# The first batch's last two token tiles in 64 by 64 tiles, and two steps moved ahead of the projection's second part

## The chip, the cores and the metric

The kernel runs on one core of a Trainium2 chip. The metric is device time in microseconds, of the whole launch; lower is better. TensorE (PE in the profile), VectorE (DVE), ScalarE (ACT) and GpSimd (POOL) each work through a queue of their own in program order and wait for each other by semaphores; SyncE (SP) issues most of the DMAs.

## What is computed

An attention whose keys and values are first squeezed to 32 slots, followed by a mixture of eight experts of which each token takes the best one:

```python
a = softmax(phi, over the sequence)                  # (8 batches, 8 heads, 576, 32)
k_m = einsum('bhsm,bhsd->bhmd', a, k)                # 32 slots per head
v_m = einsum('bhsm,bhsd->bhmd', a, v)
attn = softmax(q @ k_m.T / 8)                        # (8, 8, 576, 32)
x = (attn @ v_m) as (4608 tokens, 512)
logits = normalized(x) @ normalized(expert_emb).T / tau
e = argmax(logits); gate = softmax(logits)[e]
out = gate * (relu(x @ w1[e]) @ w2[e])               # w1 (8, 512, 1024), w2 (8, 1024, 512)
```

All is float32.

## The kernel before, in words

The eight batches are worked off one after the other by `batch` (L821), called from L1069. A batch has 576 tokens in five tiles of 128 that start at 0, 128, 256, 384 and 512 (the last has 64, and holds them twice). The 8 heads lie in two groups g of four, 32 slots each, so a group fills 128 partitions.

The attention weights of a batch stand in `aw` (slot by token). `attend` (L108) multiplies them with `vv`, which holds per head the products of values with each other and with the eight expert vectors: the columns of the experts, added over heads, are the logits, and the other columns serve the norm of a token. In batch 0 `attend` makes a 128-row matmul per tile and group (L119), `turned` (L166) transposes the tile's weights by PE and ACT copies them to `ea`, DVE adds the logits (L124), and `best` (L157) finds the maximum and the one-hot `oh`. `norm` (L175) multiplies and sums on DVE. In the later batches `open` and `pairs` (L127, L131) do the same products in 64 by 64 tiles, four per tile and group into four PSUM tiles, with 72 columns each; there the logits lie in two halves (h) that are added (L154), the transposed weights come by DMA, and the norm sums lie in two halves `s2`.

`choose` votes for the batch's most frequent expert and loads its w1. `project` (L655) multiplies the squeezed values with w1, in two halves k of 512 columns: 16 small matmuls, cast by ACT to `gh`, and the rest subtracted by DVE to `gl`. `part` (L637) splits `aw` in the same way, high part by ACT, low part by POOL. `first` (L670) is the first layer: 16 steps, for two halves s of the tokens and eight blocks f of 128 hidden units, six matmuls each (L681), then ACT's relu (L684, for s = 1 a second one, L686) and DVE's rest `hl` (L687), which is the last to read the step's PSUM tile. `mm` hands out four PSUM tiles in rotation, `pt` four others. Blocks f 0 to 3 need only the first half of `gh` and `gl`. `second` (L692) is the second layer, 40 places in eight-step tiles: tile 4 first, with h4 and w2 in float32 (L723), then tiles 0 to 3 with the split weights `wh`, `wl` (L734).

`split_w` (L648) makes one of the eight weight halves `wh` (cast) and `wl` (POOL subtract, L652).

The order of everything around these loops is written by hand: `steps` (L743) fills lists `first[n]` and `second[n]` with calls that are issued after the n-th step, in the order in which they were appended. For batch 0 before the change: weight splits 0 and 1 in first[2], splits 2 to 7 in first[9] to first[14] (the first six on POOL alone, 6 and 7 with ACT's cast); tiles 3 and 4 in first[2], their norm in first[3], the count `total` in first[4], the six parts of `late` (root of the norm, gates) in first[3] to first[8]. Of these six the first is L238, L38 and L39 on DVE, the next three are three operations each of the root, with two more in the fourth, the fifth is L254 to L256, and the sixth is ACT's exponential L258, DVE's L261 and L262, POOL's write of `idx` (L263) and three more on DVE. The scores of batch 1 come in first[9]. The softmax of batch 2's phi (two maxima L457 on DVE, two exponentials L472 on ACT) is at second[18] and second[21] of batch 0, ahead of `visit` at second[24], which transposes it (`flip`, L497) and then makes batch 1's products.

Ahead of the first layer of batch 0 the order is: first half of the projection, `part` for tokens 128 to 287, keys and values of batch 1, tiles 1 and 2 with their transposes, second half of the projection, `part` for tokens 288 to 575, norm of tiles 1 and 2.

Of the kernel before, what the change touches and what calls it, by code (L numbers as in the profile page):

```python
# [8 lines left out]
F32 = mybir.dt.float32  # L9
# [37 lines left out]
class Tokens:  # L47


    def __init__(self, k, b, pt):  # L50
        self.k, self.nc, self.b, self.pt = k, k.nc, b, pt
        wk = k.wk.tile
        self.lg = wk([P, NT, E], F32, tag="lg", name=f"lg{b}")
        self.ss = wk([P, NT], F32, tag="ss", name=f"ss{b}")
        self.s2 = wk([P, 2, NT], F32, tag="s2", name=f"s2{b}") if b else None
        self.m = wk([P, NT], F32, tag="m", name=f"m{b}")
        self.oh = wk([P, NT, E], BF16, tag="oh", name=f"oh{b}")
        self.po = {}
# [49 lines left out]
    def attend(self, *ti, pt=None, turned=True):  # L108

        k, nc, b = self.k, self.nc, self.b  # L110
        if b:
            self.open()
            self.pairs()
            return
        for i in ti:
            self.po[i] = po = (pt or self.pt)([P, NC * (D + E)], f"po{b}_{i}")
            to = slice(T0[i], T0[i] + P)
            for g in range(NG):
                nc.tensor.matmul(po[:, 144 * g : 144 * g + P + E], lhsT=k.aw[:, g, to], rhs=k.vv[:, g], start=True, stop=True)  # L119
        if turned:  # L120
            self.turned(*ti)
        for i in ti:
            e = self.po[i].rearrange("p (g m) -> p g m", g=NG)[..., D : D + E]
            nc.vector.tensor_reduce(out=self.lg[:, i], in_=e.rearrange("p g e -> p e g"), axis=AX.X, op=ALU.add)  # L124
        self.best(*ti)

    def open(self):  # L127

        self.ps = [self.pt([P, 512], f"po{self.b}_{n}") for n in range(4)]

    def pairs(self):  # L131
# [3 lines left out]
        for i in range(NT):  # L135
# [11 lines left out]
        self.room = ps[-1][:, 512 - E :]  # L147
        l2 = k.wk.tile([P, NT, E], F32, tag="l2", name=f"l2{b}")
        for n, i in enumerate((slice(0, 3), slice(3, NT))):
# [4 lines left out]
        nc.vector.tensor_tensor(out=self.lg, in0=self.lg, in1=l2, op=ALU.add)  # L154
        self.best(*range(NT))
# [19 lines left out]
    def norm(self, *ti):  # L175
        k, nc = self.k, self.nc
        for i in ti:
            x = k.ea[:, i].rearrange("p (g k m) -> p g k m", g=NG, k=2)
            po = self.po[i] if self.b else [self.po[i].rearrange("p (g k m) -> p g k m", g=NG, k=2)[..., :D]]
            for h, y in enumerate(po):  # L180
                to = x[:, :, h] if self.b else x
# [8 lines left out]
                    accum_out=(self.s2[:, h] if self.b else self.ss)[:, i : i + 1],  # L190
# [42 lines left out]
    def root(self):  # L233
        k, nc, b, ss = self.k, self.nc, self.b, self.ss
        self.n = n = k.wk.tile([P, NT], F32, tag="n", name=f"n{b}")
        if b:
            nc.vector.tensor_tensor(out=ss, in0=self.s2[:, 0], in1=self.s2[:, 1], op=ALU.add)
# [38 lines left out]
class Kernel:  # L276
# [466 lines left out]
    def steps(self, b, t, u):  # L743
# [7 lines left out]
        if not b:  # L751
            late = t.late()
            first[2].append(lambda: t.attend(3, 4))
            first[3].append(lambda: t.norm(3, 4))
            first[4] += [t.total, lambda: self.load_kv(2)]

            for f in range(3, 9):
                first[f].append(lambda: next(late))
            first[12] += [lambda: self.keep(0), lambda: self.load_q(2)]
        if u:  # L760
# [19 lines left out]
            if m < B:  # L780
                for g in range(NG):
                    second[11 + 3 * g + o].append(lambda g=g: self.softmax(m, (g,)))
# [38 lines left out]
    def batch(self, b, t, u):  # L821
# [11 lines left out]
        for k, _ in enumerate(self.project(b, self.vT[b % 2]) if u else ()):  # L833
            if not b:
                for g in range(NG):
                    self.part(g, slice(HS, S) if k else slice(P, HS), self.nc.scalar.copy)
                if k:
                    t.norm(1, 2)
                else:
                    self.keys(1)  # L840
                    self.values(1)
                    t.attend(1, 2)
        if b and u:

            self.scores(b + 1)
# [255 lines left out]
```

## Time and profile before

| | us |
|---|---|
| median of 3 runs | 406.81 (405.87 to 408.75) |
| the profiled execution | 406.74 |
| its span, first to last instruction | 404.9 |
| PE busy | 393.5 (97% of the span) |
| DVE busy | 262.3 (65%) |
| POOL busy | 171.2 (42%) |
| ACT busy | 157.2 (39%) |

The granted TensorE clock of the profiled execution is 0.998 of full. The span and the engine times come from the page's first part. Times in rows are us from the start of the span. A row of a timeline has start, duration, engine, line, operation, tile written and tiles read, the shape, how many equal instructions are merged in it, and in brackets the idle time before it with what ended it. Matmuls overlap, so a merged row lasts a little longer than the distance to the next one.

### The profile page before, as it was taken

The page shows a single profiled execution, that of the slowest core. Times are in us where ns is not written, and L with a number is a line of the kernel's source. Part 1 is how long each engine was busy: PE and PEld are TensorE (multiplying, and loading weights), DVE is VectorE, ACT ScalarE, POOL GpSimd, SP SyncE. Part 2 cuts the span into 40 slices and gives each one's busy share as a digit, 9 for nine tenths or more (in the row PEclk, how much of TensorE's full clock was granted, in tenths as well). Part 3 has the DMA queues.
Part 4 walks back from the last instruction along what each step waited for, and adds up shares of the span by engine and source line. Part 5 has one row for each costly group of instructions (what it writes and reads, how often), then busy time and mean ns, then how long its engine had stood idle before and what let it go on. Part 6 is the DMA issues. An engine that isn't in the chain of part 4 may idle for free. (4 is left out here: it accounts for less than half of the span.)

```text
span 404.9 us, 10350 instructions
## 1 busy us (share of the span) xinstructions
PE 393.5 (97%) x3933; PEld 318.5 (79%) x3933; DVE 262.3 (65%) x909; ACT 157.2 (39%) x430; POOL 171.2 (42%) x205
## 2 busy tenths in 40 slices
PE   7889999999999999999999999999999999999995
PEld 3458877798777978879787888879788897879784
DVE  4698795769664794758855795747936595745000
ACT  4366623165313633147311753137231561146110
POOL 1036563187133940369121961349303681329300
PEclk9999999999999999999999999999999999999999
DMA  8999927995679925995469926798359404790011
GB/s 265 345 363 357 375 61 183 342 358 212 149 255 386 349 46 132 346 384 234 74 215 389 387 82 160 251 388 338 56 137 361 178 2 81 249 396 6 14 53 56
DMA packets 69862, 91.24 MB, mean 225 GB/s; under 512 B 41800, under 2 KB 47688, under 8 KB 69808
## 3 DMA queue, kind: packets, MB, share of 16 engines
q1 hardware_dynamic: 66928, 82.00, 60.9%
q0 software_dynamic: 2688, 8.26, 5.8%
q8 instruction: 32, 0.52, 0.5%
q10 hardware_dynamic: 192, 0.28, 0.2%
q14 instruction: 22, 0.18, 0.1%
HBM read 71.19 MB, written 19.33 MB: 224 GB/s over the span
## 5 line engine op out<-in xcount | busy, mean ns | idle before, releaser
L681 PE MATMUL ph<-aT,gh 128*128 128x288 f32 x512 | 103.2, 297 | 0.0
L734 PE MATMUL py<-wh,hh 128*128 128x512 f32 x248 | 99.3, 400 | 0.0
L734 PE MATMUL py<-wh,hl 128*128 128x512 f32 x248 | 96.7, 390 | 0.0
L734 PE MATMUL py<-wl,hh 128*128 128x512 f32 x248 | 96.7, 390 | 0.0
L652 POOL TENSOR_TENSOR wl<-w2s,wh 128x512 fp32r<-128x512 f32 x64 | 85.1, 1330 | 5.0
L681 PEld LDWEIGHTS ph<-aT,gh 128*128 128x128 f32 x512 | 81.8, 188 | 1.7 <-DVE oh L162 0.8
L681 PE MATMUL ph<-aT,gl 128*128 128x288 f32 x256 | 75.4, 294 | 0.0
L687 DVE SCALAR_TENSOR_TENSOR hl<-ph,hh 128x288 fp32r<-128x288 f32 x128 | 55.8, 450 | 22.1 <-ACT hh L684 16.7
L739 ACT ACTIVATE ys<-py,gate 128x512 f32<-128x512 f32 (+1 forms) x39 | 25.1, 642 | 105.3 <-PE py L734 70.3
L684 ACT ACTIVATE hh<-ph 128x288 fp32r<-128x288 f32 x128 | 52.4, 417 | 31.9 <-PE ph L681 31.6
L868 POOL DMA_DIRECT2D out_dram<-ys x28 | 15.5, 553 | 106.1 <-ACT ys L739 69.4
L734 PEld LDWEIGHTS py<-wh,hh 128*128 128x128 f32 x248 | 46.5, 188 | 14.6 <-issue 4.9
L734 PEld LDWEIGHTS py<-wh,hl 128*128 128x128 f32 x248 | 46.6, 188 | 10.1
L734 PEld LDWEIGHTS py<-wl,hh 128*128 128x128 f32 x248 | 46.6, 188 | 9.0
L681 PEld LDWEIGHTS ph<-aT,gl 128*128 128x128 f32 x256 | 48.0, 188 | 0.0
L642 POOL TENSOR_TENSOR aT<-aw,aT 128x576 fp32r<-128x576 f32 (+3 forms) x20 | 23.7, 1204 | 48.4 <-DVE aT L641 42.8
L651 POOL CAST wh<-w2s 128x512 fp32r<-128x512 f32 x62 | 38.6, 622 | 1.0 <-DMA w2s<-w 0.9
L723 PE MATMUL py<-w2s,h 128*64 128x256 f32 x256 | 29.4, 382 | 0.0
L665 DVE TENSOR_TENSOR gl<-pg,gh 128x512 fp32r<-128x512 f32 x32 | 20.0, 684 | 8.7 <-ACT gh L664 8.7
L723 PEld LDWEIGHTS py<-w2s,h 128*64 128x64 f32 x256 | 17.7, 137 | 9.3 <-DVE hl L687 1.0
L472 ACT ACTIVATE ex<-ex,nm 128x576 f32<-128x576 f32 x16 | 12.3, 771 | 29.5 <-DVE nm L457 29.5
L664 ACT CAST gh<-pg 128x512 fp32r<-128x512 f32 x32 | 16.5, 599 | 10.5 <-PE pg L662 10.5
(180 smaller groups left out, 468.9 us busy)
## 6 DMA issues: line engine op xcount, KB each, us to landing
kx<-kv SPq DMA_DIRECT2D x32, 512.0 KB, 7.5
w2s<-w SPq DMA_DIRECT2D x32, 512.0 KB, 9.8
w1s<-w SPq DMA_DIRECT2D x28, 512.0 KB, 6.4
out_dram<-ys POOLq DMA_DIRECT2D x28, 256.0 KB, 6.1
qt<-qT SPq DMA_DIRECT2D x12, 576.0 KB, 8.8
ad<-aw SPq DMA_DIRECT2D x8, 576.0 KB, 12.5
td<-x SPq DMA_DIRECT2D x56, 72.0 KB, 2.1
ea<-td SPq DMA_DIRECT2D x7, 512.0 KB, 4.4
```

The costliest lines, as they stand in the source:

```text
L642: self.nc.gpsimd.tensor_tensor(out=al, in0=a, in1=ah.bitcast(F32), op=ALU.subtract)
L651: (copy or self.nc.scalar.copy)(h, x)
L652: self.nc.gpsimd.tensor_tensor(out=l, in0=x, in1=h.bitcast(F32), op=ALU.subtract)
L664: nc.scalar.copy(self.gh[:, g, f], ps[g])
L665: nc.vector.tensor_tensor(out=self.gl[:, g, f], in0=ps[g], in1=self.gh[:, g, f].bitcast(F32), op=ALU.subtract)
L681: nc.tensor.matmul(p, lhsT=w[:, g, fs], rhs=x[:, g, to], start=g == 0 and k == 0, stop=g == 1 and k == 2)
L684: nc.scalar.activation(self.hh[:, f, to], p, AF.Relu)
L687: nc.vector.scalar_tensor_tensor(out=self.hl[:, f, to], in0=p, scalar=0.0, in1=self.hh[:, f, to].bitcast(F32), op0=ALU.max, op1=ALU.subtract)
L723: nc.tensor.matmul(p[64 * j : 64 * j + 64], lhsT=self.h4[:, f], rhs=self.w2s[:, f, d * j : d * j + d], start=f == 0, stop=f == 7,)
L734: nc.tensor.matmul(p, lhsT=h[:, f, to], rhs=w[:, f], start=f == 0 and k == 0, stop=f == 7 and k == 2)
L739: nc.scalar.activation(y[:, :d], p, AF.Copy, scale=gate[:, i : i + 1])
L868: eng.dma_start(self.out[r : r + P], y)
```

## The change

Batch 0's tiles 3 and 4 go through `open` and `pairs`, which now can begin at tile 3 (two PSUM tiles instead of four), so their products become sixteen 64 by 64 matmuls of 72 columns; the transposes for `ea` follow them. Their logits are two halves that DVE adds (L154), their norms four operations instead of two, and the root begins with an addition of the two halves of `s2`. The calls for tiles 3 and 4, their norm, the count and the six parts of `late` each move one place later, to first[3], first[4], first[5] and first[4] to first[9]. The weight splits stay where they were.

The opening of batch 0 becomes: `part` of group 0 for tokens 128 to 287, first half of the projection, `part` of group 1, keys and values, products and logits of tiles 1 and 2; then step 0 of the first layer, the transposes and norms of tiles 1 and 2, step 1, the second half of the projection, `part` for tokens 288 to 575, step 2 and so on.

In batch 0 the two maxima of batch 2's softmax go to first[13] and first[14] and its exponentials to second[2] and second[5]; in the later batches the softmax is called one place earlier.

```diff
--- before.py
+++ after.py
@@ -52,7 +52,7 @@
         wk = k.wk.tile
         self.lg = wk([P, NT, E], F32, tag="lg", name=f"lg{b}")
         self.ss = wk([P, NT], F32, tag="ss", name=f"ss{b}")
-        self.s2 = wk([P, 2, NT], F32, tag="s2", name=f"s2{b}") if b else None
+        self.s2 = wk([P, 2, NT], F32, tag="s2", name=f"s2{b}")
         self.m = wk([P, NT], F32, tag="m", name=f"m{b}")
         self.oh = wk([P, NT, E], BF16, tag="oh", name=f"oh{b}")
         self.po = {}
@@ -108,9 +108,14 @@
     def attend(self, *ti, pt=None, turned=True):
 
         k, nc, b = self.k, self.nc, self.b
-        if b:
-            self.open()
-            self.pairs()
+        if b or ti[0] == 3:
+            self.open(b)
+            if b:
+                self.pairs()
+            else:
+                self.pairs(1)
+                self.turned(*ti)
+                self.logits(1)
             return
         for i in ti:
             self.po[i] = po = (pt or self.pt)([P, NC * (D + E)], f"po{b}_{i}")
@@ -124,15 +129,15 @@
             nc.vector.tensor_reduce(out=self.lg[:, i], in_=e.rearrange("p g e -> p e g"), axis=AX.X, op=ALU.add)
         self.best(*ti)
 
-    def open(self):
-
-        self.ps = [self.pt([P, 512], f"po{self.b}_{n}") for n in range(4)]
-
-    def pairs(self):
+    def open(self, all=True):
+
+        self.ps = [self.pt([P, 512], f"po{self.b}_{n}") if all or n > 1 else None for n in range(4)]
+
+    def pairs(self, first=0):
 
         k, nc, b, d, ps = self.k, self.nc, self.b, D + E, self.ps
         at = lambda i, h: ps[2 * (i // 3) + h][:, 2 * d * (i % 3) :][:, : 2 * d].rearrange("p (g m) -> p g m", g=NG)
-        for i in range(NT):
+        for i in range(3 * first, NT):
             for g in range(NG):
                 for h, c in ((0, 0), (1, 0), (0, 1), (1, 1)):
                     r, to = slice(64 * h, 64 * h + 64), slice(64 * c, 64 * c + 64)
@@ -145,14 +150,22 @@
                     )
             self.po[i] = [at(i, h)[..., E * h :][..., :D] for h in range(2)]
         self.room = ps[-1][:, 512 - E :]
+        if not first:
+            self.logits()
+
+    def logits(self, first=0):
+
+        k, nc, b, d, ps = self.k, self.nc, self.b, D + E, self.ps
         l2 = k.wk.tile([P, NT, E], F32, tag="l2", name=f"l2{b}")
-        for n, i in enumerate((slice(0, 3), slice(3, NT))):
+        for n in range(first, 2):
+            i = slice(3, NT) if n else slice(0, 3)
             for h, to in enumerate((self.lg, l2)):
                 e = ps[2 * n + h][:, : 2 * d * (i.stop - i.start)].rearrange("p (i g m) -> p i m g", g=NG, m=d)
                 e = e[:, :, D - D * h :][:, :, :E]
                 nc.vector.tensor_reduce(out=to[:, i], in_=e, axis=AX.X, op=ALU.add)
-        nc.vector.tensor_tensor(out=self.lg, in0=self.lg, in1=l2, op=ALU.add)
-        self.best(*range(NT))
+        i = slice(3 * first, NT)
+        nc.vector.tensor_tensor(out=self.lg[:, i], in0=self.lg[:, i], in1=l2[:, i], op=ALU.add)
+        self.best(*range(3 * first, NT))
 
     def best(self, *ti):
 
@@ -176,9 +189,10 @@
         k, nc = self.k, self.nc
         for i in ti:
             x = k.ea[:, i].rearrange("p (g k m) -> p g k m", g=NG, k=2)
-            po = self.po[i] if self.b else [self.po[i].rearrange("p (g k m) -> p g k m", g=NG, k=2)[..., :D]]
+            two = isinstance(self.po[i], list)
+            po = self.po[i] if two else [self.po[i].rearrange("p (g k m) -> p g k m", g=NG, k=2)[..., :D]]
             for h, y in enumerate(po):
-                to = x[:, :, h] if self.b else x
+                to = x[:, :, h] if two else x
                 nc.vector.tensor_tensor_reduce(
                     out=to,
                     in0=y,
@@ -187,7 +201,7 @@
                     scalar=0.0,
                     op0=ALU.mult,
                     op1=ALU.add,
-                    accum_out=(self.s2[:, h] if self.b else self.ss)[:, i : i + 1],
+                    accum_out=(self.s2[:, h] if two else self.ss)[:, i : i + 1],
                 )
 
     def count(self, pt, name, ti):
@@ -233,8 +247,8 @@
     def root(self):
         k, nc, b, ss = self.k, self.nc, self.b, self.ss
         self.n = n = k.wk.tile([P, NT], F32, tag="n", name=f"n{b}")
-        if b:
-            nc.vector.tensor_tensor(out=ss, in0=self.s2[:, 0], in1=self.s2[:, 1], op=ALU.add)
+        i = slice(0 if b else 3, NT)
+        nc.vector.tensor_tensor(out=ss[:, i], in0=self.s2[:, 0, i], in1=self.s2[:, 1, i], op=ALU.add)
         nc.vector.tensor_scalar(out=ss, in0=ss, scalar1=0.0, scalar2=None, op0=ALU.max)
         for _ in sqrt(nc, k.wk, n, ss, [P, NT], "nr"):
             yield
@@ -750,11 +764,11 @@
             at.append(lambda j=j: self.split_w(self.nc.gpsimd.tensor_copy if b or j < 6 else None))
         if not b:
             late = t.late()
-            first[2].append(lambda: t.attend(3, 4))
-            first[3].append(lambda: t.norm(3, 4))
-            first[4] += [t.total, lambda: self.load_kv(2)]
-
-            for f in range(3, 9):
+            first[3].append(lambda: t.attend(3, 4))
+            first[4] += [lambda: t.norm(3, 4), lambda: self.load_kv(2)]
+            first[5].append(t.total)
+
+            for f in range(4, 10):
                 first[f].append(lambda: next(late))
             first[12] += [lambda: self.keep(0), lambda: self.load_q(2)]
         if u:
@@ -779,7 +793,9 @@
             m = b + 2
             if m < B:
                 for g in range(NG):
-                    second[11 + 3 * g + o].append(lambda g=g: self.softmax(m, (g,)))
+                    if not b:
+                        first[13 + g].append(lambda g=g: self.largest(m, g))
+                    second[10 + 3 * g if b else 2 + 3 * g].append(lambda g=g: self.softmax(m, (g,)))
                 second[16 + o].append(lambda: self.shares(m))
                 second[17 + o].append(lambda: self.visit(u, m))
                 second[(20 if b else 19) + o].append(lambda: self.gather(u, m))
@@ -830,19 +846,22 @@
         if b and u:
             self.keys(b + 1)
             self.values(b + 1)
-        for k, _ in enumerate(self.project(b, self.vT[b % 2]) if u else ()):
-            if not b:
-                for g in range(NG):
-                    self.part(g, slice(HS, S) if k else slice(P, HS), self.nc.scalar.copy)
-                if k:
-                    t.norm(1, 2)
-                else:
-                    self.keys(1)
-                    self.values(1)
-                    t.attend(1, 2)
-        if b and u:
-
-            self.scores(b + 1)
+        project = self.project(b, self.vT[b % 2]) if u else ()
+        if b:
+            list(project)
+            if u:
+                self.scores(b + 1)
+        else:
+            self.part(0, slice(P, HS), self.nc.scalar.copy)
+            next(project)
+            self.part(1, slice(P, HS), self.nc.scalar.copy)
+            self.keys(1)
+            self.values(1)
+            t.attend(1, 2, turned=False)
+            first[0] += [lambda: t.turned(1, 2), lambda: t.norm(1, 2)]
+            first[1].insert(0, lambda: list(project))
+            for g in range(NG):
+                first[1].append(lambda g=g: self.part(g, slice(HS, S), self.nc.scalar.copy))
         for n, _ in enumerate(self.first(b)):
             for step in first[n]:
                 step()
```

## Rows read from the trace of the kernel before

**Rows 1.** Waits of PE, 26 to 66 us: engine, line, releaser, total, times, longest.
```profile
PE po L504 <- ACT ex L472: 0.5, 1, 0.5
PE tt L172 <- ACT kT L551: 0.4, 1, 0.4
PE pg L662 <- DMA w1s<-w: 0.3, 1, 0.3
```

**Rows 2.** Windows: stretch, length, busy us (count) of five engines, clock, DMA, GB/s.
```profile
150.00:200.00 50.00, 50.00 (x507) 41.32 (x506) 35.16 (x119) 19.25 (x52) 21.39 (x24) 1.00 0.74 239
```

**Rows 3.** Timeline of PE in the opening, 29 to 37 us.
```profile
29.32 1.09 PE L119 MATMUL po<-vv,aw 128*128 128x136 f32 x8
30.77 0.66 PE L172 MATMUL tt<-ident,aw 128*128 128x128 f32 x4 [0.36 <-ACT kT L551]
31.36 1.09 PE L662 MATMUL pg<-w1s,vT 64*32 64x512 f32 x16
...
34.86 1.09 PE L119 MATMUL po<-vv,aw 128*128 128x136 f32 x8
35.78 0.60 PE L172 MATMUL tt<-ident,aw 128*128 128x128 f32 x4
36.14 0.51 PE L681 MATMUL ph<-aT,gh 128*128 128x288 f32 x2
```

**Rows 4.** Timeline of PE at steps 8 and 9 of the first layer.
```profile
40.83 0.43 PE L681 MATMUL ph<-aT,gh 128*128 128x288 f32 x2
...
41.23 0.52 PE L681 MATMUL ph<-aT,gh 128*128 128x288 f32 x2
```

**Rows 5.** Timeline of DVE, 33 to 41 us.
```profile
33.14 1.29 DVE L665 TENSOR_TENSOR gl<-pg,gh 128x512 fp32r<-128x512 f32 x2 [0.91 <-ACT gh L664]
...
36.61 0.92 DVE L162 TENSOR_TENSOR oh<-lg,m 128x16 bf16<-128x16 f32 x1
...
38.83 0.63 DVE L238 TENSOR_SCALAR ss<-ss 128x5 f32<-128x5 f32 x1
...
39.70 0.17 DVE L39 TENSOR_SCALAR nrg<-nrg 128x5 int32<-128x5 int32 x1
...
40.71 0.45 DVE L687 SCALAR_TENSOR_TENSOR hl<-ph,hh 128x288 fp32r<-128x288 f32 x1
```

**Rows 6.** Timeline of POOL, 34 to 45 us.
```profile
34.00 1.57 POOL L642 TENSOR_TENSOR aT<-aw,aT 128x288 fp32r<-128x288 f32 x2 [2.70 <-ACT aT L641]
...
36.22 1.28 POOL L652 TENSOR_TENSOR wl<-w2s,wh 128x512 fp32r<-128x512 f32 x1
...
38.13 1.30 POOL L652 TENSOR_TENSOR wl<-w2s,wh 128x512 fp32r<-128x512 f32 x1
44.50 0.20 POOL L263 TENSOR_SCALAR idx<-m 128x5 f32<-128x5 f32 x1 [5.07 <-DVE m L262]
```

**Rows 7.** Timeline of PE where batch 0 turns batch 2's softmax, 64 to 66 us.
```profile
64.40 0.28 PE L504 MATMUL po<-ident,ex 64*128 64x64 f32 x2 [0.46 <-ACT ex L472]
...
65.10 1.48 PE L139 MATMUL po<-vv,aw 64*64 64x72 f32 x80
```

**Rows 8.** Timeline of DVE, the two maxima of batch 2's softmax.
```profile
61.98 1.37 DVE L457 TENSOR_REDUCE nm<-ex 128x1 f32<-128x576 f32 x2
```

**Rows 9.** Timeline of DVE, norms of batch 1 in two halves.
```profile
71.86 0.28 DVE L182 CUSTOM_DVE_ANT_1 ea<-po,ea 128x128 f32<-128x128 f32 x1
...
72.07 0.28 DVE L182 CUSTOM_DVE_ANT_1 ea<-po,ea 128x128 f32<-128x128 f32 x1
```

**Rows 10.** Timeline of DVE, one operation of two SBUF inputs at two places.
```profile
140.97 1.12 DVE L73 TENSOR_TENSOR x<-x,mx 128x576 f32<-128x576 f32 x1
...
145.19 0.75 DVE L73 TENSOR_TENSOR x<-x,mx 128x576 f32<-128x576 f32 x1
```

**Rows 11.** Timeline of POOL, the cast beside the first of them.
```profile
140.85 0.61 POOL L651 CAST wh<-w2s 128x512 fp32r<-128x512 f32 x1
```

**Rows 12.** Timeline of ACT, the exponential of batch 0's gates.
```profile
43.74 0.24 ACT L258 ACTIVATE l<-l 128x40 f32<-128x40 f32 x1 [1.79 <-DVE l L256]
```

## The prediction

> **What bounds the kernel now.** I read the waits of TensorE (PE) first. From 26 to 66 us PE stands still three times, 0.5, 0.4 and 0.3 us [rows 1]; after that it is full, as the window from 150 to 200 us shows [rows 2] (the next three windows of 50 us read the same). So the kernel runs as long as PE's own queue, and whatever PE gains or loses in the first batch comes out at the end one to one. Then I read PE's timeline of the opening [rows 3] and around steps 8 and 9 of the first layer [rows 4] (a step is one pass of L681 over six matmuls; 16 per batch, 0 to 15). One thing in rows 4 matters: the pair of matmuls at 41.23 takes 0.52 us where the pair before it takes 0.43. The 0.1 us is a small wait that the waits view does not list. Step 9 writes the PSUM buffer that step 5 used (four in rotation), and VectorE (DVE) reads step 5's buffer at 40.71 for 0.45 us, until 41.16 [rows 5]. So at step 9 DVE is already just late: PE has no slack against DVE there. Last I read DVE beside GpSimd (POOL): the one-hot compare L162 lasts 0.92 us and the maximum L238 0.63 [rows 5], where L39, of the same shape as L238, takes 0.17. Both long ones lie under a POOL subtract L652 and end with it: 37.53 against 37.50, 39.46 against 39.43 [rows 5, 6]. Two engines wait for each other here.
>
> **The change, part by part, on PE.** *Opening.* The products of tiles 1 and 2 start at 29.32 as before and take 0.92 us (by the equal block at 34.86, which gives way to transposes at 35.78) [rows 3]. Before, the transposes then wait 0.36 us for ACT's copy of kT and start at 30.77. Now step 0 stands there, at 30.24. Its last operand, POOL's low part of group 1, starts when ACT has cast group 1, which stays behind two gh casts; I allow 0.1 to 0.2 us. A step costs 0.80 (two spacings of 0.40 in rows 4) and 0.1 more when another kind of matmul stood before it (0.51 against 0.43, at 36.14 and 40.83 [rows 3, 4]). So: step 0 to 31.2, transposes 0.4 to 31.6, step 1 to 32.5, second part of the projection (1.0, plus 0.1) to 33.6, steps 2 and 3 to 35.3.
>
> *Products of tiles 3 and 4.* Eight records in 0.92 become 32. The same shape appears in batch 1: 80 records in 1.48 [rows 7], so 32 take 0.59; with nothing for the changes of shape the gain is 0.33, with two restarts of 0.1 it is 0.13. I take 0.17, nearer the second, since the block stands between two other shapes. Then transposes 0.36: step 4 starts at 36.45, before at 36.14 + 0.9 = 37.0. PE has gained 0.5 to 0.6. (The Trainium skill, TensorEngine Tiling (Array Packing), Tiling Modes, promises four independent 64 by 64 tiles and says that a change of mode drains the engine. At the full four tiles the products would take 0.92 x 72/136 = 0.49, an estimate from that page, and save 0.43; the row says 0.59 before any drain.)
>
> *First batch's softmax for batch 2.* The two maxima (L457, 1.37 us for both) run at 61.98, directly behind DVE's last transpose into aw [rows 8]; PE waits 0.46 us for the exponentials at 64.40 [rows 7]. Put into steps 13 and 14 and the start of the second layer, they are done some 10 us earlier, so the 0.46 goes. What is late next there is the aw that the products at 65.10 read: DVE has it at about 62, so over 3 us are left, and where DVE is late PE is late too. The cost is 1.4 us of DVE at steps 13 to 15, covered: PE needs those buffers four allocations on. For the later batches the move by one place changes no engine's own order: nothing of DVE, ACT or POOL stands between the two places. I cost it at nothing both ways. The phi it reads is loaded long before; no DMA moves past another on SP.
>
> **The change on DVE and POOL.** This is the costly part.
>
> *DVE.* The second half of gl started at 33.14, 1.78 us behind its projection at 31.36, and took 1.29 [rows 3, 5]. The projection now starts at 32.6, so gl runs 34.4 to 35.65. hl of steps 2 and 3 (0.4 each and queued behind ACT's two casts of `part`; 0.45 with the overlap [rows 5]) follow to 36.6, two short reduces to 36.85. Every short operation I count at 0.2, by L39's 0.17 and a gap. From there the queue is: add of l2 (new), max, one-hot, hl 4, four norms (0.21 each, by the starts 71.86 and 72.07 [rows 9]; two longer ones before), add of s2 (new), L238, L38, L39, hl 5.
>
> *POOL.* Its parts of columns 288 to 575 started at 34.00 for 1.57 us [rows 6], 0.86 behind gl; now 35.2 to 36.75. Then cast 0.61 [rows 11], subtract 1.28 [rows 6], twice: 36.75 to 37.35, to 38.7, to 39.35, to 40.7. Before, POOL then sat 5.07 us waiting to write idx at 44.50 [rows 6]. idx belongs to the sixth late step, which moves from step 8 to step 9, and in step 9 the third weight split is issued ahead of it. So a third cast and subtract now run at once, 40.75 to 41.35 and 41.45 to 42.75, under the root's small operations.
>
> *Together.* Each operation of DVE with two SBUF inputs, as L162, or of L238's kind waits for POOL's running one; L38 and L39 are of L238's kind and I let them wait too. That a cast holds DVE as well shows in L73: 1.12 us at 140.97 under the cast of 140.85, 0.75 at 145.19 [rows 10, 11]. So: add 36.9, free at 37.2, done 37.4; max; one-hot asked at 37.65, free 38.55, done 38.75; hl 4 to 39.15; norms to 40.05; add of s2 asked at 40.1, done 40.75; L238 done 41.4; L38 slips in between; L39 asked at 41.65, done 42.8; hl 5 done 43.3. Waits: 0.3 + 0.9 + 0.5 + 0.4 + 1.1 = 3.2 us, where before there were 0.75 + 0.45 = 1.2.
>
> Step 9 of PE is due at 40.6 (41.13 without its small wait, less the 0.55) but cannot start before 43.35; it started at 41.23 [rows 4]. **PE loses 2.1 us there** and all of the opening's gain.
>
> *ACT.* The exponential L258 waited 1.79 us in ACT's queue at 43.74 [rows 12]. It now stands behind step 9's relu and ahead of the four copies out of the scores. It waits for DVE's l, at 46.9 by the same walk (three or four short operations and an hl per step: hl 6 at 44.2, hl 7 at 45.1, hl 8 at 46.4). The copies (0.25 each, an estimate from L258's 0.24) end at 48.1, relu and hl of step 10 at 49.0, and step 14, due at 48.65, needs that buffer: 0.35 us more.
>
> **Sum.** 2.1 + 0.35 - 0.46 = 2.0 us. The profiled execution took 406.74 us (span 404.9), beside a median of 406.81: they agree, so 406.74 + 2.0 = **408.7 us**.
>
> (The Trainium skill, SBUF — State Buffer, Who interferes with whom, speaks against this change: DVE and GpSimd share one port pair as an exclusive lock held for a whole instruction, and it names two SBUF inputs and the two-port mode of `tensor_scalar` and casts. The trace agrees with 0.92 and 0.63 us. By that rule L38 and L39 wait too and the time comes out at the 408.7; no row shows these two beside a busy POOL.)
>
> **Rivals.** *The integer operations L38 and L39 do not wait.* Then hl 5 ends at 42.2, step 9 starts at 42.25, 1.0 late; ACT's exponential then costs 0.6 at step 14: +1.6 - 0.46, 407.9 us. For it: they work on int32, L238 on f32. Against: same operation and shape.
>
> *Faster: DVE is in time.* If hl 5 is done by 40.6, PE keeps its 0.5, the 0.1 of step 9 and the 0.46: 405.7 us. With no port wait at all the walk has hl 5 at 40.8, and 0.3 + 0.46 gives 406.0. It decides at step 9: every 0.1 us of hl 5 behind 40.6 is 0.1 lost. For it: the waits are short if POOL's splits start later than I place them. Against: hl 5 had no slack before, and DVE's queue only grows.
>
> *The change misses at the flip.* The transposes at 64.40 wait for something else that is late with DVE: the 0.46 stays, 409.2 us. Against: aw is there over 3 us ahead [rows 7, 8].
>
> *The clock.* PE would stand about 2.2 us before step 9, longer than any wait in rows 1. The granted clock was 1.00 (2.4 GHz) in the windows I read [rows 2]; if it fell to 1.2 GHz after such a pause, matmuls would take twice as long for some us: about 410.5.
>
> **Chances.** DVE late through the port, L38 or L39 included: 0.45. Without them: 0.25. In time: 0.2. Flip: 0.05. Clock: 0.05. The range 405.7 to 409.8 holds all but the last and the tails of runs (405.87 to 408.75 for one kernel); the likeliest alone 408.1 to 409.4. About 1% is what a measurement of this kernel can tell from no change, 4 us here: all cases but accidents are inside. Faster 0.01, same 0.95, slower 0.04.
>
> **What would show it.** Right: step 9 starting near 43.3 with PE idle ahead of it; L39 or its neighbour lasting over 1 us under a POOL subtract; POOL's third split ahead of idx; no wait at the flip. Wrong in the port: L162, L238 and the new adds at 0.2 us each. Wrong in the opening: step 0 starting later than 30.5, or step 4 later than 36.8. A forecast of slower falls if step 9 starts before 41.

## The result and the profile after

The changed kernel takes 409.34 us (median of 22 runs, 408.03 to 410.53), the kernel before 406.69 on the same chip (22 runs, 405.61 to 408.75): a ratio of 1.0058, 95% interval 1.0046 to 1.0070. It is slower by 2.65 us, where 2.0 were forecast. The profiled execution took 409.43 us (span 407.6, before 404.9), so its 2.7 us more can be followed along PE's timeline. The marks of both executions, as starts of the same work on PE:

| mark on PE | before | after | shift |
|---|---|---|---|
| first projection | 27.80 | 27.07 | -0.73 |
| step 9 of the first layer | 41.23 | 42.90 | +1.67 |
| second layer of batch 0 | 48.47 | 50.38 | +1.91 |
| flip, first transposes of te | 64.51 | 65.90 | +1.39 |
| first layer of batch 1 | 83.35 | 85.03 | +1.68 |
| projection of batch 2 | 128.03 | 129.82 | +1.79 |
| projection of the last batch | 357.87 | 359.67 | +1.80 |
| end of PE | 400.00 | 402.66 | +2.66 |

So 1.9 us arise in the first layer of batch 0, 0.5 come back at the flip, 0.3 are added at batch 1's projection, 0.1 behind it, and 0.9 in the last projection. The places behind the flip were not in the forecast. The 0.73 us at the first projection are no gain that lasts: PE starts when w1 has landed, anywhere from 26.96 to 28.92 us in the kernels below, and after the early start it waits for DVE's transpose L92 into aw, which ends at 29.24 us here and at 29.15 before (the row at 29.30 below). PE's waits after, from 26 to 70 us (columns as in [rows 1]; lines behind the first edit are shifted by up to 19 against the kernel before, hl L687 is L701 now):

```profile
PE ph L695 <- DVE hl L701: 1.5, 1, 1.5
PE pg L676 <- DMA w1s<-w: 0.8, 1, 0.8
PE all L212 <- DVE oh L175: 0.4, 1, 0.4
PE po L124 <- DVE aw L92: 0.2, 1, 0.2
```

The wait for the exponentials at the flip and the one for kT of [rows 1] are gone; one of 1.5 us for hl has come, and one of 0.4 for the one-hot, ahead of the count's matmuls. PE's timeline after, which answers to [rows 3, 4]: six of the products of tiles 1 and 2, step 0, the products of tiles 3 and 4 (sixteen in the program, 32 records in the trace) with their transposes, step 4, the second half of step 8, step 9, step 14:

```profile
29.30 0.96 PE L124 MATMUL po<-vv,aw 128*128 128x136 f32 x6 [0.15 <-DVE aw L92]
30.01 0.52 PE L695 MATMUL ph<-aT,gh 128*128 128x288 f32 x2
...
35.30 0.73 PE L144 MATMUL po<-vv,aw 64*64 64x72 f32 x32
35.96 0.66 PE L185 MATMUL tt<-ident,aw 128*128 128x128 f32 x4
36.37 0.51 PE L695 MATMUL ph<-aT,gh 128*128 128x288 f32 x2
...
40.83 0.43 PE L695 MATMUL ph<-aT,gh 128*128 128x288 f32 x2
42.90 0.54 PE L695 MATMUL ph<-aT,gh 128*128 128x288 f32 x2 [1.51 <-DVE hl L701]
...
48.58 0.54 PE L695 MATMUL ph<-aT,gh 128*128 128x288 f32 x2
```

PE is at step 4 0.6 us sooner than before (at 37.01 there) and stands still ahead of step 9. DVE at the same time, beside [rows 5]:

```profile
36.79 0.50 DVE L167 TENSOR_TENSOR lg<-lg,l 128x16 f32<-128x16 f32 x1
...
37.53 1.12 DVE L175 TENSOR_TENSOR oh<-lg,m 128x16 bf16<-128x16 f32 x1
...
39.90 0.68 DVE L251 TENSOR_TENSOR ss<-s 128x2 f32<-128x2 f32 x1
40.61 0.53 DVE L252 TENSOR_SCALAR ss<-ss 128x5 f32<-128x5 f32 x1
41.17 0.17 DVE L38 TENSOR_SCALAR nrg<-ss 128x5 int32<-128x5 int32 x1
41.38 1.11 DVE L39 TENSOR_SCALAR nrg<-nrg 128x5 int32<-128x5 int32 x1
42.40 0.44 DVE L701 SCALAR_TENSOR_TENSOR hl<-ph,hh 128x288 fp32r<-128x288 f32 x1
```

And POOL, beside [rows 6]:

```profile
36.65 0.62 POOL L665 CAST wh<-w2s 128x512 fp32r<-128x512 f32 x1
37.34 1.28 POOL L666 TENSOR_TENSOR wl<-w2s,wh 128x512 fp32r<-128x512 f32 x1
...
39.26 1.29 POOL L666 TENSOR_TENSOR wl<-w2s,wh 128x512 fp32r<-128x512 f32 x1
40.50 0.61 POOL L665 CAST wh<-w2s 128x512 fp32r<-128x512 f32 x1
41.19 1.27 POOL L666 TENSOR_TENSOR wl<-w2s,wh 128x512 fp32r<-128x512 f32 x1
47.11 0.20 POOL L277 TENSOR_SCALAR idx<-m 128x5 f32<-128x5 f32 x1 [4.65 <-DVE m L276]
```

Read the two together by their ends. L167 ends at 37.29, the first cast at 37.27; L175 ends at 38.65, the first subtract at 38.62; L251 at 40.58 with the second subtract at 40.55; L252 at 41.14 with the third cast at 41.11; L39 at 42.49 with the third subtract at 42.46. L38, of L39's shape and type, slipped in at 41.17, before the subtract had begun, and took 0.17. Against 0.17 each the five are 3.1 us longer.

### The profile page after: what moved, and what is told of

Its sections match the earlier page's. It is cut to its first block, busy times and chain, and to the rows that moved or that the text cites. A ratio compares the mean times of both kernels' runs of the same rounds, so it can differ in the third digit from the quotient of the medians.

```text
span 407.6 us, 10405 instructions
## 1 busy us (share of the span) xinstructions
PE 395.9 (97%) x3957; PEld 319.4 (78%) x3957; DVE 263.2 (65%) x915; ACT 157.5 (39%) x430; POOL 170.8 (42%) x205
## 5 line engine op out<-in xcount | busy, mean ns | idle before, releaser
L701 DVE SCALAR_TENSOR_TENSOR hl<-ph,hh 128x288 fp32r<-128x288 f32 x128 | 55.9, 450 | 22.0 <-ACT hh L698 17.7
```

The source lines that it names most:

```text
L701: nc.vector.scalar_tensor_tensor(out=self.hl[:, f, to], in0=p, scalar=0.0, in1=self.hh[:, f, to].bitcast(F32), op0=ALU.max, op1=ALU.subtract)
```

## The experiments

Each was compared with the kernel before on its own chip; ratios are against it.

**Third split behind idx** (the changed kernel with one exchange in step 9):

```diff
-            for f in range(4, 10):
+            for f in range(4, 9):
                 first[f].append(lambda: next(late))
+            first[9].insert(0, lambda: next(late))
```

> The changed kernel, with one exchange in step 9: the sixth piece of the root and gates (it holds the write of idx on GpSimd) is issued ahead of the third weight split instead of behind it. Theory (shared port): GpSimd then stands waiting for idx while VectorE runs the maximum L252 and the integer operation L39, so L252 falls from 0.53 to about 0.17 us and L39 from 1.11 to about 0.17; hl of step 5 ends near 41.6 instead of 42.85, step 9 starts near 41.6 instead of 42.9, and the time is about 1.3 us below the changed kernel: 408.0. Rival (VectorE is late simply because it has more operations; what GpSimd does beside it doesn't matter): L252 and L39 keep their lengths or step 9 stays at 42.9 and the time at 409.3. Second rival (the later splits are what the second layer then waits for): step 9 near 41.6, but the 128x512 products of the second layer wait for wl, and the time is 408.5 or more.

Measured: 409.86 us against 406.56, ratio 1.0075 (1.0058 to 1.0093). The waits under the root went as the port theory has it; from DVE's timeline of this kernel:

```profile
41.15 0.17 DVE L252 TENSOR_SCALAR ss<-ss 128x5 f32<-128x5 f32 x1
...
41.56 0.17 DVE L39 TENSOR_SCALAR nrg<-nrg 128x5 int32<-128x5 int32 x1
...
53.19 1.79 DVE L73 TENSOR_TENSOR x<-x,mx 128x576 f32<-128x576 f32 x1
...
56.50 1.51 DVE L73 TENSOR_TENSOR x<-x,mx 128x576 f32<-128x576 f32 x1
```

The whole edit lies behind step 4, so that is where to count from: step 4 starts at 36.92, step 9 at 42.14, 5.22 us between, 6.53 in the changed kernel (36.37 to 42.90). That is 1.31 us less; 1.3 were expected. But the time did not fall to 408.0, and neither did the second rival come true as it was put: no product waits for wl. The splits that were pushed behind idx now run under L73, the subtract of batch 1's attention, 1.79 and 1.51 us where the changed kernel shows 1.10 and 0.76. What comes of it stands in SP's timeline (DMA issues: td of batch 1, later w1), first of this kernel, then of the changed one:

```profile
59.99 5.81 SPq L100 DMA_DIRECT2D td<-x  x8
...
73.88 2.12 SPq L456 DMA_DIRECT2D w1s<-w  x4
```

```profile
59.31 5.81 SPq L100 DMA_DIRECT2D td<-x  x8
...
71.17 2.97 SPq L456 DMA_DIRECT2D w1s<-w  x4
...
349.23 2.60 SPq L456 DMA_DIRECT2D w1s<-w  x4
```

PE reaches batch 1's projection 0.75 us sooner (80.65 against 81.40) and finds w1 issued 2.7 us later. PE's weight loads of this kernel at that place:

```profile
82.52 0.14 PEld L676 LDWEIGHTS pg<-w1s,vT 64*32 64x32 f32 x4 [1.72 <-DMA w1s<-w]
83.59 0.18 PEld L676 LDWEIGHTS pg<-w1s,vT 64*32 64x32 f32 x16 [0.92 <-DMA w1s<-w]
```

From the projection to the first layer of batch 1 it takes 5.87 us here, 3.63 in the changed kernel: the gain is given back there, with more. That td and w1 are late because of L73 is read from the order of the queues, not shown by a run of its own; in the next kernel L73 takes 0.78 and 1.51 us, and w1 is issued at 71.16, no later than in the changed kernel.

**First three splits behind idx**:

```diff
-            at = first[j] if b else first[2] if j < 2 else first[7 + j]
-            at.append(lambda j=j: self.split_w(self.nc.gpsimd.tensor_copy if b or j < 6 else None))
+            at = first[j] if b else first[9] if j < 2 else first[7 + j]
+            at.append(lambda j=j: self.split_w(self.nc.gpsimd.tensor_copy if b or j < 4 else None))
```

with the sixth late piece ahead of them as above.

> The changed kernel with the first three weight splits all issued behind idx, so that GpSimd has no split under the one-hot compare and the root's small operations; to make up for it, ScalarE takes over the casts of splits 4 and 5 (numbered from 0) as it does those of 6 and 7. Theory (shared port): the add of l2, the one-hot compare, the add of s2, L252 and L39 take about 0.2 us each, VectorE is some 3 us earlier, hl of step 5 is done by 40.8 and step 9 starts by 41.0; PE is 2 us ahead of the changed kernel at the second layer: about 407.2 us if the splits are in time there, and up to 1.2 us more if the last ones (ready near 57.5, wanted near 56.5) are late. Rival (more operations, not the port): step 9 stays within 0.4 us of 42.9 and the time is 409 or more.

Measured: 409.67 us against 406.56, ratio 1.0087 (1.0061 to 1.0113). DVE's and PE's timelines of it:

```profile
36.99 0.17 DVE L167 TENSOR_TENSOR lg<-lg,l 128x16 f32<-128x16 f32 x1
...
37.40 0.18 DVE L175 TENSOR_TENSOR oh<-lg,m 128x16 bf16<-128x16 f32 x1
...
39.42 0.16 DVE L251 TENSOR_TENSOR ss<-s 128x2 f32<-128x2 f32 x1
...
40.02 0.17 DVE L39 TENSOR_SCALAR nrg<-nrg 128x5 int32<-128x5 int32 x1
```

```profile
27.92 1.09 PE L676 MATMUL pg<-w1s,vT 64*32 64x512 f32 x16 [0.80 <-DMA w1s<-w]
...
36.57 0.51 PE L695 MATMUL ph<-aT,gh 128*128 128x288 f32 x2
...
40.87 0.43 PE L695 MATMUL ph<-aT,gh 128*128 128x288 f32 x2
...
57.68 0.50 PE L748 MATMUL py<-wl,hh 128*128 128x512 f32 x1 [0.79 <-POOL wl L666]
```

All five operations take 0.16 to 0.18 us (L252 0.17) and step 9 (40.87) waits for nothing. The rival "more operations, not the port" has fallen: the operations are the same, and 2.2 us went with the splits (4.30 us from step 4 to step 9, against 6.53; before, 4.22). But the time is above the 407.2 to 408.4 that were expected. The price comes in the second layer: two waits for wl of 1.1 us together, and from its start to the flip 17.58 us, against 15.52 in the changed kernel. Batch 1's projection takes 3.85 us, 0.2 more. From the first projection to step 9 it is 12.95 us, 13.43 in the kernel before (27.80 to 41.23), with the two projections starting 0.12 us apart: 0.48 gained, the gain of the new opening that the forecast put at 0.5 to 0.6.

**The new order alone** (the kernel before, with the changed kernel's `steps` and `batch` but the softmax in its old place):

> The kernel before with the new order alone: the second part of the projection behind two steps, the norms and the six late pieces one step later, but the products of tiles 3 and 4 as before and the softmax where it was. It has neither the add of l2 nor the add of s2, but the third split is again ahead of idx. Theory (shared port): the one-hot compare comes about 0.4 us earlier and meets the first cast rather than the first subtract, L238 and L39 wait together about 1 us; step 9 starts between 41.0 and 42.0, the wait at the flip stays at 0.46: 406.4 to 407.6 us, 407.1 the likeliest. Rival (the order alone costs the 2 us, through the later gl and the later norms): step 9 at 42.7 or later, 408.5 us or more. Rival (the order alone is a gain of 0.5): step 9 before 40.8, 406.2.

Measured: 407.13 us against 406.56, ratio 1.0014 (1.0003 to 1.0024), the likeliest value of the expectation. Its waits of PE from 26 to 70 us and three rows of DVE:

```profile
PE ph L681 <- DVE hl L687: 1.2, 2, 0.6
PE pg L662 <- DMA w1s<-w: 0.9, 1, 0.9
```

```profile
39.09 1.19 DVE L38 TENSOR_SCALAR nrg<-ss 128x5 int32<-128x5 int32 x1
40.31 0.52 DVE L39 TENSOR_SCALAR nrg<-nrg 128x5 int32<-128x5 int32 x1
...
41.39 0.79 DVE L43 SCALAR_TENSOR_TENSOR nrr<-nrr,ss 128x5 f32<-128x5 f32 x1
```

Step 9 started at 41.24, in the expected span; a second wait of 0.6 us came at step 14, at 47.55 (two expectations below call it step 12). Against the expectation the wait at the flip did not stay: the two lines above are all of PE's waits from 26 to 70 us, though the softmax stands at its old place. From the second layer to the flip it takes 15.48 us, 16.04 before. Here it is L38 that waits, under the second subtract (38.95 to 40.25): which of the small operations pays depends on where a split happens to stand.

**The 64 by 64 products alone** (the kernel before, with `Tokens` of the changed one):

> The kernel before with the products of tiles 3 and 4 in 64 by 64 tiles alone (32 instead of 8, with the adds of l2 and s2 on VectorE that follow from it); order, softmax and places of the late pieces as before. Theory (shared port): the products save 0.15 to 0.2 us of PE; the add of l2 comes at about 36.6 under the first weight subtract of GpSimd (36.2 to 37.5) and waits for its end, the one-hot compare behind it then meets the second cast or subtract, and VectorE is 1 to 2 us later at hl of step 5: step 9 starts at 42 to 43, the time is 407.5 to 408.5. Rival (the two adds cost only their own 0.2 us each): step 9 at 41.5, the time 406.8 to 407.0. Rival (the pairs are a plain gain): 406.5.

Measured: 408.07 us against 406.56, ratio 1.0033 (1.0016 to 1.0051). The time was in the expected span, the place was not. L167 does wait (1.09 us at 36.71), but the one-hot compare behind it then takes 0.31, so hl of step 5 ends at 40.73, and step 9 at 41.73 waits for nothing. PE loses 0.3 us between step 4 and step 9 all the same (4.55 us, 4.22 before), 0.2 of them where the count waits for the one-hot. From the products' start to step 3 it takes 1.08 us (35.23 to 36.31), before 1.28 (34.86 to 36.14 [rows 3]): 0.2 saved, as forecast. Another 0.3 us lies in the last batch (see PE's instruction stream below); the rest, some 0.7 us, among it a wait of 0.5 for w1 in the opening, stays open, with 12 runs that go from 406.2 to 410.4.

**The softmax alone**:

```diff
-                    second[11 + 3 * g + o].append(lambda g=g: self.softmax(m, (g,)))
+                    if not b:
+                        first[13 + g].append(lambda g=g: self.largest(m, g))
+                    second[10 + 3 * g if b else 2 + 3 * g].append(lambda g=g: self.softmax(m, (g,)))
```

> The kernel before with the move of the softmax alone (the two maxima into steps 13 and 14 of the first batch, the exponentials to the start of its second layer, one place earlier in the later batches). Theory (the 0.46 us at the flip goes, the maxima are covered): PE has no wait at the flip, the time is 406.2 us against 406.6 to 406.7. Rival (the gain is given back on the way of batch 1: the maxima stand ahead of VectorE's transposes and subtracts of batch 1's attention, so td, ea and the load of w1 start later by 0.5 us or more, and the projection of batch 1 waits longer for w1 than its 0.2 us): no wait at the flip, more wait at the projection near 80 us, the time 406.6 or more.

Measured: 406.16 us against 407.08, ratio 0.9978 (0.9963 to 0.9993). PE's only wait from 26 to 70 us is `pg L662 <- DMA w1s<-w: 0.3`; the flip has none. So this part is a gain by itself; L73 took 1.39 and 1.51 us, and w1 of batch 1 was not later. Its 0.9 us is more than the wait of 0.46; of the rest 0.3 us stood at batch 1's projection (2.97 us in place of 3.30), which takes 2.97 in before_fetch below too, where the softmax did not move. The gain does not add to others: see the candidates below.

**PE's instruction stream.** In the last batch the changed kernel's projection waits 0.74 us for w1, the kernel before not at all:

```profile
360.57 0.57 PEld L676 LDWEIGHTS pg<-w1s,vT 64*32 64x32 f32 x18 [0.74 <-DMA w1s<-w]
```

The loads are issued by SP, and the second of the four took 1.00 us after and 0.35 before. The tile view of w1s gives the shortest, median and longest issue in ns, after and then before:

```profile
L456 SPq DMA_DIRECT2D w1s<-w x4: 332/348/997, 349.2 to 351.5; - x4
```

```profile
L442 SPq DMA_DIRECT2D w1s<-w x4: 332/342/365, 347.4 to 349.1; - x4
```

This is the 2.60 in SP's timeline above, and before:

```profile
347.44 1.96 SPq L442 DMA_DIRECT2D w1s<-w  x4
```

The DMA view of just these stretches has one line more after: a transfer of instructions (16 KB, by the page's 32 packets of 0.52 MB), from 349.54 to 350.49, in the middle of that issue (349.79 to 350.78). In the kernel before this queue's nearest transfers start at 342.0 and 361.5.

```profile
q8 instruction: 1, 0.02, 2.3%
```

All four kernels with the 32 products and no padding, and so 24 matmuls and 24 weight loads more in PE's stream, show such a transfer at 348.4 to 350.4 and a second issue of 0.85 to 1.00 us; the kernels without them (and without the padding below) show neither. Two runs tell whether it is the length of the stream. The one adds 24 matmuls to the kernel before, of about the same columns in all (35 of 160 for 11 of 512), where nothing depends on them:

```diff
-    k.warm(11)
+    k.warm(35, hot=k.mm([P, 512], "hot", 0)[:, :160])
```

> The kernel before with 35 warm-up matmuls of 160 columns in place of the 11 of 512 at the very start of PE: the same columns, but 24 matmuls and 24 weight loads more in PE's instruction stream, as the changed kernel has 24 more matmuls (32 for 8) further on. Nothing else differs. Theory (the instruction stream): PE's 16 KB fetch of instructions, which in the last batch fell at 342.0 and 361.5 us, now falls near 348, while SyncE issues the four loads of w1; the second of these takes 0.85 to 1.0 us in place of 0.35, the last projection waits 0.2 to 0.7 us for w1, and the time is 0.3 to 0.8 us above the kernel before: 407.0 to 407.5. Rival (the long issue has to do with the changed products or buffers): the second issue of w1 takes 0.35 us, no wait there, the time 406.6.

Measured: 407.69 us against 407.08, ratio 1.0026 (1.0007 to 1.0046). SP's and PE's rows of the last batch:

```profile
346.25 2.64 SPq L442 DMA_DIRECT2D w1s<-w  x4
```

```profile
357.37 0.57 PEld L662 LDWEIGHTS pg<-w1s,vT 64*32 64x32 f32 x18 [0.52 <-DMA w1s<-w]
```

The second issue took 1.03 us, the transfer starts at 346.6, and the end shifts by 0.7 us between the last projection and the layer behind it. The other run is the changed kernel with 20 matmuls more (31 of 180 columns):

> The changed kernel with 31 warm-up matmuls of 180 columns in place of the 11 of 512: 40 more entries in PE's instruction stream, so that its fetches fall some us earlier and the one of 349.5 us lands ahead of the loads of w1 of the last batch. Theory (the instruction stream): the second issue of w1 in the last batch takes 0.35 us again, the wait of 0.7 us at the last projection goes, and the time is 0.5 to 0.9 us below the changed kernel: 408.5 to 408.8, if no fetch falls upon another load that PE waits for. Rival: 409.3, with the wait of 0.7 us still there.

Measured: 408.17 us against 407.08, ratio 1.0025 (1.0007 to 1.0042); the changed kernel has 1.0058 (1.0046 to 1.0070).

```profile
348.79 1.96 SPq L456 DMA_DIRECT2D w1s<-w  x4
```

The second issue takes 0.35 again and the last projection waits for nothing (mark 359.23 to end 401.36: the shift stays at 1.36). Batch 1's projection takes 2.97 us here, 3.63 in the changed kernel. The transfer of instructions starts at 347.7 here and is over when SP begins to issue. Both runs went as the theory of the stream had it, this one by more than the 0.5 to 0.9 us expected, since batch 1's projection fell too. Why a transfer of instructions makes a DMA issue of SP longer is not shown.

**Third split ahead of idx in the kernel before**:

```diff
-            at = first[j] if b else first[2] if j < 2 else first[7 + j]
+            at = first[j] if b else first[2] if j < 2 else first[8 if j == 2 else 7 + j]
```

> The kernel before with one exchange: the third weight split is issued in step 8 ahead of the sixth late piece, so ahead of idx on GpSimd, and runs at once (cast near 39.5 to 40.1, subtract near 40.2 to 41.5) under the root's small operations. The suspected cause alone, in the old kernel. Theory (shared port): L39 at 39.7 waits for the cast (0.4 us in place of 0.17), L43 of the first round waits for the subtract (0.2 to 0.8), hl of step 5 ends about 0.4 us later and step 9 with it, hl 6 and 7 likewise: PE loses 0.3 to 0.6 us before the second layer. After it the splits end 2 us earlier and VectorE's subtracts of batch 1's attention wait less, which is worth nothing to PE unless w1 of batch 1 was late. Time 0.2 to 0.5 us above the kernel before. Rival (GpSimd's running instruction doesn't hold 128x5 operations): step 9 at its old place, the time as before.

Measured: 406.33 us against 406.70, ratio 0.9993 (0.9978 to 1.0008). The waits came where they were expected:

```profile
38.65 0.51 DVE L38 TENSOR_SCALAR nrg<-ss 128x5 int32<-128x5 int32 x1
...
39.93 0.60 DVE L43 SCALAR_TENSOR_TENSOR nrr<-nrr,ss 128x5 f32<-128x5 f32 x1
```

PE waited 0.3 us at step 9 and lost 0.8 between step 4 and step 9 in all (4.99 us, 4.22 before), more than the 0.3 to 0.6 expected. But the time is the same: L73 fell to 0.89 and 0.76 us (1.56 and 1.51 before), the wait at the flip went, though the softmax had not moved (PE's list of waits has only 0.4 us for w1, 0.4 for kT and 0.3 for hl; 15.52 us from the second layer to the flip, 16.04 before), and batch 1's projection took 0.3 us less. Some 0.8 us moved from one place to others.

**Three candidates.** The changed kernel without the 64 by 64 products, third split behind idx:

> A candidate for a better version: the changed kernel without the 64 by 64 products of tiles 3 and 4 (so without the adds of l2 and s2), with the new order and the moved softmax, and with the third weight split behind idx. Theory (shared port): L38, L39 and L43, which in order_only took 1.19, 0.52 and 0.79 us, fall to 0.2 except where the second split still runs; step 9 starts within 0.3 us of PE's own time, the second wait of 0.6 us at step 12 goes, and so does the wait at the flip: 1.2 + 0.46 us below order_only's 407.1, 405.6 us. Rival (the splits that are pushed behind idx meet VectorE's subtracts of batch 1's attention instead, which delays the load of w1 of batch 1): a wait of 0.5 to 2 us at the projection near 80 us, the time 406.2 to 407.5.

Measured: 408.21 us against 407.08, ratio 1.0024 (1.0004 to 1.0045): the rival, with a time above its 406.2 to 407.5. One wait of 0.3 us for hl is left, but L73 takes 1.79 and 1.52 us and PE's weight loads wait 1.69 us for w1 at batch 1's projection. The same with the third split ahead of idx:

> The changed kernel without the 64 by 64 products of tiles 3 and 4 (new order and moved softmax, the third split ahead of idx as in the change). What it lacks against the changed kernel is the pairs' share; what it has against order_only is the moved softmax alone. Theory: the waits for hl of order_only (0.6 us at step 9 and 0.6 at step 12) stay, the wait at the flip goes, the subtracts L73 of batch 1's attention take 1.25 and 0.76 us as there, so w1 of batch 1 is issued in time, and PE's fetch of instructions stays out of the last batch's loads of w1 as in order_only: 406.7 us, 0.4 below order_only and 1.5 below order_softmax, which differs only in where the third split stands. Rival (the third split ahead of idx is worse than behind): 408.2 or more.

Measured: 407.38 us against 406.70, ratio 1.0018 (1.0000 to 1.0036). The hl waits stayed (1.2 us), as expected, but the time is neither 1.5 us below the one before it nor, within the intervals, below order_only: this expectation fell. Against the changed kernel it is 0.4% faster, about 1.6 us, and that is the share of the products in 64 by 64 tiles; their two adds on DVE and the stream's length would make it up. And the kernel before with the softmax and the third split ahead:

> A candidate that should beat both kernels: the kernel before with the moved softmax and with the third weight split ahead of idx (nothing of the new order, no 64 by 64 products of tiles 3 and 4). Theory: the wait of 0.46 us at the flip goes; the third split costs PE 0.3 us at step 10, as in third_ahead, and gives VectorE back more than 1 us in batch 1's attention (L73 at 0.8 to 0.9 us), so that the two maxima delay nothing: between softmax_only's ratio and 0.3 us less, 405.6 to 406.2 us against a median of 406.6 to 407.1 for the kernel before. Rival (the third split's 0.3 us at step 10 is a plain loss, because w1 of batch 1 was not late in softmax_only either): 406.5 to 406.8, no gain that can be measured over the kernel before.

Measured: 406.57 us against 406.59, ratio 0.9997 (0.9981 to 1.0013): no gain. Its third split costs PE a wait of 0.3 us, as in third_ahead, at step 9 and not at step 10. Of all versions only softmax_only beats both kernels, by 0.2% over the one before. Twice the softmax was moved beside another change, and twice no gain can be seen: no_pairs has 1.0018 where order_only has 1.0014, softmax_third 0.9997 where third_ahead has 0.9993. The traces give a reason: in order_only and third_ahead the flip no longer waits, so there was no wait left to take away.

## Why the prediction was right or wrong

**Right, as forecast and shown.** *The port.* L39 on int32 waits like its f32 neighbour (1.11 us under the third subtract), so the rival without L38 and L39 fell. The five waits are 3.1 us in all, 3.2 forecast; the one-hot ends at 38.65 (38.75 forecast), hl of step 5 at 42.84 (43.3), step 9 starts at 42.90 (43.35). That POOL's splits cause it is shown by the run without them. *The opening.* Step 0 at 30.01 (30.24), step 4 at 36.37 (36.45). Step 0 is sooner by some luck: in the early start two of the eight products ran ahead of the wait for aw. *The flip.* 0.5 us back, but third_ahead and order_only show that the wait also goes when the splits or PE's steps shift, without the softmax. *The clock.* Granted 1.00 from 35 to 60 us (2.4 GHz), in spite of the pause of 1.5 us.

**Mis-sized.** Step 9 is 1.67 us late, not 2.1. From step 4 to step 9 it takes 6.53 us (6.54 in after_fetch), 6.90 forecast: POOL's splits ran sooner than they were placed (the third subtract to 42.46, not 42.75, which is where L39 ends), and hl follows L39 more closely. *ACT's exponential*: L272 ran at 46.35 (46.9 forecast), step 14 waits 0.1 us, and from step 9 to the second layer it takes 0.24 us more than before (7.48 against 7.24); 0.35 was forecast. By the end of the first layer the forecast was 0.5 us too high. Two readings of the walk were 0.1 to 0.2 off, without weight in the sum. Step 9's own time was 41.23 and not 41.13, since its row starts 0.40 us behind the one before it like the others; the 0.1 us lies inside the step. And the add of l2 and the one-hot are let go at 37.2 and 38.55, where the walk's own times for POOL end the cast at 37.35 and the subtract at 38.7.

**Missing.** The step that failed is the costing of the products of tiles 3 and 4: "Eight records in 0.92 become 32" counts the 24 more matmuls and loads as time on PE (0.17 us saved; 0.2 measured), not as length of PE's program. The 0.9 us of the last batch has its cause there, as the two runs with padded warm-up show; without it the time would be about 408.5 in place of 409.3, an estimate from the marks. The +0.3 at batch 1's projection (its wait for w1 went from 0.2 to 0.5 us) was not foreseen either; in the other kernels this place takes 2.97 to 5.87 us, so w1 of batch 1 has hardly any slack, and what part of the 0.3 belongs to the change is not settled.

So it is in part luck that the time came within 0.7 us of the forecast: two errors of opposite sign, 0.5 too much in the first layer and 1.3 too little behind the flip. "Whatever PE gains or loses in the first batch comes out at the end one to one" did not hold in general: in third_behind a gain of 1.3 us at step 9 was lost whole at 80 us, where PE waited for w1.

## What to carry to other kernels

Where two engines hold each other for whole instructions, moving the long one away from a row of short ones can merely change who pays, as it did in four kernels here: look up what it will stand beside at its new place before the move is made. Count a change that adds instructions to the fullest queue also as a shift of that engine's later instruction fetches, and look at what runs on the DMA queues where they will fall. And test a bundle's parts one by one, then in pairs: here one part was a gain by itself, and nothing beside another change that took away the same wait.

## What the runs showed of the hardware

- DVE operations of 128x5 or 128x2 elements wait for POOL's running cast or subtract to its end, on int32 as on f32, `tensor_scalar` as those with two SBUF inputs: 0.17 us alone, 0.5 to 1.2 beside it. A reciprocal did not (L42 in order_only, 0.17 us at 41.18 under a subtract that ran from 40.88 to 42.15), nor a maximum over an axis (L174 in pairs_only, 0.17 at 37.84 under a cast), nor what reads PSUM (hl, 0.44 to 0.46; norms, 0.28). The Trainium skill, SBUF — State Buffer, Who interferes with whom, names two SBUF inputs, `tensor_scalar` and casts; the rows agree, down to two elements per partition.
- A 16 KB transfer of instructions that falls into a load's issue on SP goes with an issue of 0.85 to 1.03 us in place of 0.35 (five kernels with it, eight without), and w1's median landing goes from 5.0 to 7.6 us in the last batch.
- 32 products of 64 by 64 tiles make a row of 0.73 us (0.59 was scaled from the 80 in 1.48) and the next block starts 0.66 behind them; 8 of the full array make a row of 1.09, 0.92 to the next block. With the changes of shape around them 0.2 us are saved.
